# Waits between input loads, ten places apart, and a warm-up of many short matmuls in a long-convolution and MLP kernel

## The chip, the cores and the metric

The kernel runs on one core of one Trainium2 chip. The metric is the device time of one execution in microseconds, the median over several runs. A core has five instruction streams that run side by side and meet at semaphores: TensorE (PE; its weight loads are listed apart as PEld), VectorE (DVE), ScalarE (ACT), GpSimd (POOL) and SyncE (SP). SP computes nothing here; it issues DMA transfers, which 16 DMA engines carry out.

## What is computed

Two layers, each a gated long convolution (A) and an MLP (B), on a sequence of 2048 positions with 512 channels, in bf16:

```python
def _A_ref(q, k, v, shift_k, ssm_k, ssm_D):
    ...
    for t in range(ks):
        k_shift = k_shift + k_pad[:, t:t + S, :] * shift_k[:, ks - 1 - t][None, None, :]
    kv = k_shift * v
    ...
    y_f = kv_f * kf_f[None, :, :, :]
    ...
    y = y + kv * ssm_D[None, None, :]
    return q * y

def _B_ref(x, w1, b1, w2, b2):
    y = _layernorm(x, axis=-1)
    h = _gelu(jnp.einsum("bsd,df->bsf", y, w1) + b1)
    return jnp.einsum("bsf,fd->bsd", h, w2) + b2

x = A_q
x = x + _A_ref(_layernorm(x, axis=-1), A_k, A_v, A_shift_k, A_ssm_k, A_ssm_D)
x = x + _B_ref(_layernorm(x, axis=-1), B_w1, B_b1, B_w2, B_b2)
x = x + _A_ref(_layernorm(x, axis=-1), A_k, A_v, A_shift_k, A_ssm_k, A_ssm_D)
x = x + _B_ref(_layernorm(x, axis=-1), B_w1, B_b1, B_w2, B_b2)
```

`k_shift` is a causal filter of four taps along the sequence (ks = 4). `kv_f` and `kf_f` are Fourier transforms over a sequence padded to 4096, so y is the causal convolution of kv with ssm_k. It depends on k and v alone and is the same in both layers: the kernel computes it once.

## The kernel before

The program first makes a list of operations, each with an engine, a function that issues its instructions, and the operations that it depends on (`preds`, found from the memory that each reads and writes). `Prog.arrange` puts them in the order written out by hand in `ORDER`, engine by engine. `Prog.sync` turns dependences into semaphore waits, and leaves out those that an engine knows of already. `Prog.emit` issues everything: an instruction's waits come just before it on its engine, so a wait also holds back all that stands behind it in that engine's stream. A DMA that is waited for has a semaphore of its own.

The stages that the prediction speaks of, with their lines:

- **Loads.** ScalarE's queue issues four small ones (identity and first Fourier matrix, the taps, ssm_D). All others are on SP's queue: ssm_k in four pieces of 512 KB (L467), k in eight pieces of 256 KB (L482) and two small edge pieces (L474, L476), v in eight (L482), the second Fourier table in sixteen pieces of 256 KB (`tload`, L483), one small table (L490) and the row b2 (L703). `ORDER` puts these 40 first on SP, with no wait among them. Behind them stand sixteen copies from SBUF to SBUF (L577) that wait for the h2 stage, with b1 (L704) among them, and then the tables, q, W1 and W2 for the later stages, which overwrite memory that the first stages read. The last rows of W2 (L702) go to memory that nothing used before.
- **Warm-up** (L492 to L501, `warm`): GpSimd clears a 128x512 tile, and PE multiplies it by itself eight times, 512 columns each, into a PSUM tile that nobody reads. It is the first work on PE. The taps' matmuls (L511) and the transposes of ssm_k are made to follow it.
- **ht** (L522 to L534): PE transposes each quarter of ssm_k with 16 matmuls (L528), VectorE copies the result out of PSUM (`evac`, L453), and a small add on one row follows, on VectorE for two quarters and on GpSimd for two (L450).
- **h1, h2** (stage 1, L536; stage 2, L551): the transform of ssm_k, matmuls L545 and L558, evicted by ScalarE and VectorE.
- **fir** (L581 to L632): the filter of four taps. Channel groups 0 and 1 are done on PE: transposes of k (L589), then matmuls with diagonal matrices of the taps (L606), and a product with v on VectorE (L613). GpSimd makes the eight 128x128 diagonal matrices, one tap scaling each (L520), four for each group. In GpSimd's stream they stand behind the adds of the ht stage and two memsets (L489); their order is one of group 0, one of group 1, one of group 0, one of group 1, one of group 0, two of group 1, one of group 0. Group 1's matmuls come first on PE, so they need the first seven. Channel groups 2 and 3 are done on VectorE, as products and sums of two SBUF operands with 2048 columns (L450).
- **x1, x2, i1, i2**: the transform of kv (L545), the products with that of ssm_k (L651, matmuls of 64 columns; the products on VectorE), and the two inverse stages (L674, L731).
- **The layers** (L778 on): normalization on VectorE and GpSimd, the MLP on PE (L827, L860), GELU on ScalarE (L832), transposes by DMA (L807), stores.

PE's stream is fixed by `ORDER` too. Its beginning: warm-up, transposes of two quarters of ssm_k, tap rows, transposes of a third, h1 matmuls, transposes of the fourth, h1 with the transposes of k for group 1 and group 0 in between, the FIR matmuls of group 1, and then h2.

Of the kernel before, what the change touches and what calls it, by code (L numbers as in the profile page):

```python
# [12 lines left out]
PE, ACT, DVE, POOL, SP = "tensor", "scalar", "vector", "gpsimd", "sync"  # L13
# [25 lines left out]
class Prog:  # L39
# [157 lines left out]
    def arrange(self):  # L197

        self.order = {e: [] for e in (PE, ACT, DVE, POOL, SP)}
        last = [None] * 8  # L200
        second = set(self.SECOND)
        assert sorted(self.ORDER) == list(range(len(self.ops)))
        for at, i in enumerate(self.ORDER):
            o = self.ops[i]
            o.eng = o.engs[i in second]
            o.at, o.pos = at, len(self.order[o.eng])
            self.order[o.eng].append(o)
            tl = o.tile
            if tl is not None and tl.base is None:
                tl.base = self.BANKS[tl.i]  # L210
                for b in range(tl.base, tl.base + tl.nb):
                    if last[b] is not None:
                        for p in [p for p in last[b].ops if p.eng != PE] or last[b].ops[-1:]:
                            assert p.eng is not None
                            if p.i not in o.preds:
                                o.preds[p.i] = "psum"
                    last[b] = tl
            assert all(self.ops[p].eng is not None for p in o.preds)
# [149 lines left out]
def bass_interleave_layers__ssm_conv_h3__mixer_channel_mlp__prompt_kernel(  # L368
# [7 lines left out]
    def A(p0, n, off, *dims):  # L376
        return bass.AP(ar, p0 * AR + off, [[AR, n]] + [list(d) for d in dims])
# [7 lines left out]
    def Q(tile, p0, n, off, *dims):  # L385
        return bass.AP(ps, p0 * 4096 + tile.base * 512 + off, [[4096, n]] + [list(d) for d in dims])
# [65 lines left out]
    def evac(engs, dst, src, tile):  # L452
        f = {ACT: lambda e: e.activation(dst, src(), AF.Copy), DVE: lambda e: e.tensor_copy(dst, src())}  # L453
        return P.op(engs, f, writes=[dst], tile=tile)
# [14 lines left out]
    z = A(0, 1, R_K + c0, [512, 3], [1, WDV])  # L469
# [17 lines left out]
    for i in range(NPE):  # L487
        z = A(0, 128, R_KT[i], [130, 16], [1, 2])
# [3 lines left out]
    z = A(0, 128, R_W, [1, 512])  # L492
    P.op(POOL, lambda e, z=z: e.memset(z, 0.0), writes=[z])
    P.tag = "warm"
    tl = Tile(2)

    def f(e, tl=tl, z=z):
        for i in range(8):
            r = e.matmul(Q(tl, 0, 128, 0, [1, 512]), z[:, :128], z, start=True, stop=True)
        return r  # L500
    warm = P.op(PE, f, reads=[z], tile=tl)  # L501

    one = A(0, 1, R_ONE, [1, 128])
    P.op(POOL, lambda e: e.memset(one, 1.0), writes=[one])
    P.tag = "taps"
    tl = Tile(2)
    ins = [(i, A(0, 1, R_SR + 512 * c, [1, 512])) for i, c in enumerate(DV_CH)]

    def f(e, ins=ins, tl=tl):
        for i, m in ins:  # L510
            r = e.matmul(Q(tl, 0, 128, 512 * i, [1, 512]), one, m, start=True, stop=True)  # L511
        return r
    P.op(PE, f, reads=[one] + [m for _, m in ins], tile=tl).preds[warm.i] = "psum"
    for i in range(NDV):
        evac(ACT, A(0, 128, R_SJ + i * 512, [128, 4], [1, 128]), lambda tl=tl, i=i: Q(tl, 0, 128, 512 * i, [1, 4], [4, 128]), tl)
# [6 lines left out]
    for b in range(4):  # L522
        tl = Tile(2)
# [27 lines left out]
    def stage2(G, ks, n):  # L551

        tl = Tile(2)
        ins = [(i, A(0, 128, R_S2 + k * 128, [1, 128]), A(0, 128, G + k * n, [1, n])) for i, k in enumerate(ks)]

        def f(e):
            for i, w, m in ins:
                r = e.matmul(Q(tl, 0, 128, i * n, [1, n]), w, m, start=True, stop=True)  # L558
            return r
        P.op(PE, f, reads=[x for y in ins for x in y[1:]], tile=tl)  # L560
        return tl
# [5 lines left out]
    for k8 in range(16):  # L567
        tl = stage2(R_G, range(8 * k8, 8 * k8 + 8), 128)
# [203 lines left out]
    def ntmp():  # L772
        nn[0] += 1
        return R_N + (nn[0] % 8) * 512
# [3 lines left out]
    for L in range(2):  # L778
        s0 = 0
        for n in (BLOCKS0, BLOCKS1)[L]:  # L780
# [6 lines left out]
            for i, s in enumerate(sl):  # L787
                z = ntmp()
# [12 lines left out]
            for i, s in enumerate(sl):  # L801
                z = ntmp()
# [6 lines left out]
                tl = Tile(1)  # L809
# [9 lines left out]
            for fc in range(11):  # L819
                rows = 128 if fc < 10 else 96  # L820
                tl = Tile(1)
# [13 lines left out]
            for i, s in enumerate(sl):  # L835
                P.tag = "m2"
                tl = Tile(1)
# [63 lines left out]
```

## Time and profile before

| | |
|---|---|
| time of three runs | 242.47, 241.10, 241.46 us; median 241.46 |
| profiled execution, first to last instruction | 238.8 us |
| PE busy | 226.2 us (95%), 2312 matmuls, 2332 weight loads |
| DVE busy | 171.6 us (72%) |
| ACT busy | 138.3 us (58%) |
| POOL busy | 41.3 us (17%) |
| DMA | 27.40 MB, mean 115 GB/s; 241 to 383 GB/s over the first 30 us |
| instruction packets | 18 of 16 KB on one queue, 7 of 8 KB on another |

The profile is that of one execution on the chip. Its times count from the first instruction, and its span leaves out what lies before and behind the program; the median of the runs is 2.7 us longer. In its lists a row names the line of the kernel, the engine, the operation, what is written and read, and the shapes. Rows of a timeline merge instructions of one line that follow each other closely, with a count behind the x; idle time before a row stands in brackets with what ended it. The chain of waits is followed back from the last instruction: each piece is work, or a DMA, or "issue" where an engine waited for nothing that the profile shows. The ends of matmuls are modelled, so a PE that is busy 95% of the span isn't at its peak for all of it.

### The profile page before, as it was taken

How to read it: one execution, taken by the hardware profiler on the slowest of the kernel's cores; microseconds unless marked ns; L12 is line 12 of the kernel's file. 1: busy time of each engine (PE TensorE's matmuls, PEld its weight loads, DVE VectorE, ACT ScalarE, POOL GpSimd, SP SyncE). 2: the span in 40 equal slices, each digit the busy share in tenths (PEclk: the TensorE clock that was granted, in tenths of full speed). 3: DMA queues.
4: the chain of work that ended last, by engine and by line, in shares of the span. 5: the costliest groups of instructions: out<-in, count | busy, mean ns of one | idle time of the engine just before them, and what ended most of it. 6: DMA issues, size and time to landing. Idle time of an engine off the chain costs nothing.

```text
span 238.8 us, 5555 instructions
## 1 busy us (share of the span) xinstructions
PE 226.2 (95%) x2312; PEld 151.6 (63%) x2332; DVE 171.6 (72%) x359; ACT 138.3 (58%) x225; POOL 41.3 (17%) x77
## 2 busy tenths in 40 slices
PE   7987989886999999999999999999999999999995
PEld 3875778875899886766766667644444444444543
DVE  0979999999999999999887999693793312030035
ACT  2598799999999995642754444342782042454100
POOL 2179000000013444041230310400220200000000
PEclk9999999999999999999999999999999999999999
DMA  6999949999960003111122022240013021310024
GB/s 241 364 342 383 383 148 253 249 272 309 379 227 0 3 0 68 26 23 31 37 47 44 0 48 44 45 88 3 0 22 66 3 44 31 101 44 3 0 71 148
DMA packets 37035, 27.40 MB, mean 115 GB/s; under 512 B 19506, under 2 KB 29969, under 8 KB 37010
## 3 DMA queue, kind: packets, MB, share of 16 engines
q1 hardware_dynamic: 36446, 26.91, 37.8%
q8 instruction: 18, 0.29, 0.5%
q10 hardware_dynamic: 564, 0.14, 0.4%
q14 instruction: 7, 0.06, 0.1%
HBM read 16.82 MB, written 2.10 MB: 79 GB/s over the span
## 4 chain that ended last, share of the span: by engine, by line
PE 77%; ACT 9%; DMA 4%; DVE 4%; SPq 3%; issue 3%; ACTq 0%
PE ps L860 31%; PE ps L827 30%; ACT ar L453 9%; PE ps L674 5%; PE ps L731 3%; SPq L439 3%; PE ps L545 3%; DMA ar<-in_A_ssm_k_dram 2%; DVE ar L453 2%; DMA ar<-ar 2%; PE ps L528 1%; PE ps L606 1%; PE ps L849 1%; DVE sm L754 1%; PE ps L589 1%
## 5 line engine op out<-in xcount | busy, mean ns | idle before, releaser
L832 ACT ACTIVATE ar<-ps,sm 128x256 bf16<-128x256 f32 (+4 forms) x143 | 64.7, 525 | 72.5 <-PE ps L827 68.1
L827 PE MATMUL ps<-ar 128*128 128x256 bf16 (+4 forms) x568 | 84.2, 297 | 0.2
L860 PE MATMUL ps<-ar 128*128 128x512 bf16 (+1 forms) x329 | 79.0, 379 | 0.6
L453 ACT ACTIVATE ar<-ps 128x1024 bf16<-128x1024 f32 (+1 forms) x81 | 72.5, 1057 | 9.0 <-PE ps L511 4.5
L827 PEld LDWEIGHTS ps<-ar 128*128 128x128 bf16 (+1 forms) x572 | 52.9, 100 | 29.8 <-ACT ar L832 0.5
L450 DVE TENSOR_TENSOR ar<-ar 128x512 bf16<-128x512 bf16 (+3 forms) x106 | 63.6, 634 | 2.0 <-DMA ar<-in_A_k_dram 1.3
L860 PEld LDWEIGHTS ps<-ar 128*128 128x128 bf16 (+1 forms) x341 | 33.1, 98 | 34.3 <-ACT ar L832 0.3
L864 DVE TENSOR_TENSOR ar<-ar,ps 128x512 bf16<-128x512 bf16 x31 | 20.6, 680 | 47.3 <-PE ps L860 47.3
L754 DVE BATCH_NORM_STATS2 sm<-ar 128x6 f32<-128x512 bf16 (+1 forms) x68 | 42.8, 647 | 0.1
L768 DVE TENSOR_SCALAR ar<-ar,sm 128x512 bf16<-128x512 bf16 x64 | 25.0, 407 | 7.8 <-POOL sm L762 5.2
L760 POOL TENSOR_SCALAR sm<-sm 128x2 f32<-128x2 f32 (+2 forms) x26 | 6.0, 232 | 93.9 <-DVE sm L756 93.3
L762 POOL TENSOR_TENSOR sm<-sm 128x2 f32<-128x2 f32 (+2 forms) x26 | 21.6, 832 | 2.2
L545 PE MATMUL ps<-ar 128*64 128x128 bf16 x512 | 17.1, 221 | 1.4 <-issue 0.8
L545 PEld LDWEIGHTS ps<-ar 128*64 128x64 bf16 x512 | 14.9, 110 | 3.2 <-issue 1.0
L674 PE MATMUL ps<-ar 128*128 128x128 bf16 x256 | 15.0, 220 | 0.6 <-ACT ar L453 0.6
L674 PEld LDWEIGHTS ps<-ar 128*128 128x128 bf16 x256 | 14.7, 114 | 0.8 <-ACT ar L453 0.8
L453 DVE CAST ar<-ps 128x1024 bf16<-128x1024 f32 x11 | 13.0, 1212 | 0.3 <-PE ps L558 0.3
L651 PE MATMUL ps<-ar 128*128 128x64 bf16 x256 | 9.8, 194 | 3.2 <-ACT ar L453 2.7
L453 DVE COPY ar<-ps 128x2048 bf16<-128x2048 bf16 (+1 forms) x8 | 8.2, 1024 | 6.4 <-PE ps L528 6.3
L651 PEld LDWEIGHTS ps<-ar 128*128 128x128 bf16 x256 | 8.2, 98 | 4.7 <-ACT ar L453 3.9
L756 DVE BATCH_NORM_AGGREGATE sm<-sm 128x2 f32<-128x6 f32 (+1 forms) x64 | 9.9, 171 | 0.3
L558 PE MATMUL ps<-ar 128*128 128x128 bf16 x128 | 8.6, 220 | 0.8 <-ACT ar L453 0.8
(34 smaller groups left out, 78.1 us busy)
## 6 DMA issues: line engine op xcount, KB each, us to landing
ar<-tab_s SPq DMA_DIRECT2D x16, 256.0 KB, 9.6
ar<-ar SPq DMA_DIRECT2D x16, 256.0 KB, 4.2
ar<-in_A_ssm_k_dram SPq DMA_DIRECT2D x4, 512.0 KB, 5.3
ar<-in_A_k_dram SPq DMA_DIRECT2D x8, 256.0 KB, 7.6
ar<-in_A_v_dram SPq DMA_DIRECT2D x8, 256.0 KB, 9.6
ar<-in_A_q_dram SPq DMA_DIRECT2D x4, 512.0 KB, 7.9
out_dram<-ar SPq DMA_DIRECT2D x7, 256.0 KB, 2.1
ar<-in_B_w_dram SPq DMA_DIRECT2D x1, 1376.0 KB, 12.6
```

Source lines behind the costliest of these rows:

```text
L450: return P.op(eng, lambda e: e.tensor_tensor(o, a, b, op), reads=[a, b] + list(more), writes=[o])
L453: f = {ACT: lambda e: e.activation(dst, src(), AF.Copy), DVE: lambda e: e.tensor_copy(dst, src())}
L545: r = e.matmul(Q(tl, 64 * ri, 64, i * 128, [1, 128]), w, m, start=True, stop=True)
L651: r = e.matmul(Q(tl, 0, 128, i * pitch, [1, n]), w, m, start=True, stop=True)
L674: r = e.matmul(Q(tl, 0, 128, i * 128, [1, 128]), w, m, start=q == 0, stop=q == 1)
L754: P.op(DVE, lambda e, sj=sj, x=x: e.bn_stats(sj, x), reads=[x], writes=[sj])
L762: P.op(POOL, lambda e: e.tensor_tensor(r, v, hf, ALU.pow), reads=[v, hf], writes=[r])
L768: P.op(DVE, lambda e: e.tensor_scalar(o, x, m, r, ALU.subtract, ALU.mult), reads=[x, m, r], writes=[o])
L827: r = e.matmul(Q(tl, 0, rows, 0, [1, w]), a, m, start=dk == 0, stop=dk == 3)
L832: P.op(ACT, lambda e, dst=dst, tl=tl, rows=rows, bias=bias, w=w: e.activation(dst, Q(tl, 0, rows, 0, [1, w]), AF.Gelu_apprx_tanh, bias=bia ...
L860: r = e.matmul(Q(tl, 0, 128, 0, [1, 512]), ins[fc][0], ins[fc][1], start=fc == 0, stop=fc == 10)
L864: P.op(DVE, lambda e, x=x, tl=tl: e.tensor_tensor(x, x, Q(tl, 0, 128, 0, [1, 512]), ALU.add), reads=[x], writes=[x], tile=tl)
```

## The change

Two edits; the order of all operations stays.

```diff
@@ Prog.arrange
         second = set(self.SECOND)
         assert sorted(self.ORDER) == list(range(len(self.ops)))
+        early = [i for i in self.ORDER if self.ops[i].engs == (SP,) and self.ops[i].dma and not self.ops[i].preds]
+        for i, j in zip(early, early[10:]):
+            self.ops[j].preds[i] = "raw"
         for at, i in enumerate(self.ORDER):
@@ warm-up
     def f(e, tl=tl, z=z):
-        for i in range(8):
+        for i in range(6):
             r = e.matmul(Q(tl, 0, 128, 0, [1, 512]), z[:, :128], z, start=True, stop=True)
+        for i in range(60):
+            r = e.matmul(Q(tl, 0, 128, 0, [1, 64]), z[:, :128], z[:, :64], start=True, stop=True)
         return r
```

`early` is the list of DMAs on SP's queue that depend on nothing: the 40 loads at the head of the queue, then b1 (L704) and the last rows of W2 (L702), 42 in all. Each from the eleventh on now depends on the one ten places ahead, so that SP waits until that one has landed before it issues the next. The data, their order and their sizes are the same.

The warm-up keeps six of its eight matmuls of 512 columns and gets sixty of 64 columns, each with its own weight load of the same 128x128 zeros. PE's first operation thus issues 66 pairs of weight load and matmul instead of 8.

## The prediction

> **What bounds the kernel now.** I read the chain of waits first (start, length, what; one piece per row), because the change touches only the first 35 us and the chain says what those microseconds hang on.
>
> ```profile
> 1.18 4.84 DMA ar<-in_A_ssm_k_dram
> 6.03 0.05 issue
> 6.08 1.23 PE ps L528 x16
> ...
> 20.77 1.31 issue
> 22.08 1.01 PE ps L589 x15
> 23.09 0.05 issue
> 23.15 1.69 PE ps L606 x13
> 24.84 0.46 PE ps L558 x8
> 25.30 0.02 issue
> 25.32 10.20 ACT ar L453 x11
> ```
>
> The chain leaves the loads as early as 6.03 us and is compute afterwards: transposes (L528), first-layer matmuls, FIR matmuls (L606), ScalarE evictions. It has no load in it after the second ssm_k landing. So a slower load need not matter, and a later TensorE start can. Next the timeline of PE in the first microseconds (start, length, work).
>
> ```profile
> 1.56 3.33 PE L499 MATMUL ps<-ar 128*128 128x512 bf16 x8 [1.56 <-POOL ar L493]
> 4.78 2.52 PE L528 MATMUL ps<-ar 128*128 128x128 bf16 x32
> ```
>
> The eight zero matmuls end just as the first ssm_k load lands (4.73 us): the warm-up is hidden today with nothing to spare. Then the timelines of GpSimd and VectorE, which turn out to matter most.
>
> ```profile
> 13.86 2.70 POOL L520 TENSOR_SCALAR ar<-ar,sm 128x128 bf16<-128x128 bf16 x4
> ...
> 16.81 2.36 POOL L520 TENSOR_SCALAR ar<-ar,sm 128x128 bf16<-128x128 bf16 x1
> 19.26 0.60 POOL L520 TENSOR_SCALAR ar<-ar,sm 128x128 bf16<-128x128 bf16 x1
> 19.96 2.61 POOL L520 TENSOR_SCALAR ar<-ar,sm 128x128 bf16<-128x128 bf16 x1
> 22.67 1.22 POOL L520 TENSOR_SCALAR ar<-ar,sm 128x128 bf16<-128x128 bf16 x1
> ```
>
> ```profile
> 12.79 2.35 DVE L453 CAST ar<-ps 128x1024 bf16<-128x1024 f32 x2
> 16.42 2.36 DVE L450 TENSOR_TENSOR ar<-ar 128x2048 bf16<-128x2048 bf16 x2 [1.28 <-DMA ar<-in_A_k_dram]
> 18.70 1.22 DVE L453 COPY ar<-ps 128x2048 bf16<-128x2048 bf16 x1
> 19.83 3.58 DVE L450 TENSOR_TENSOR ar<-ar 128x2048 bf16<-128x2048 bf16 x3
> 23.34 1.21 DVE L453 COPY ar<-ps 128x2048 bf16<-128x2048 bf16 x1
> 24.87 1.23 DVE L613 TENSOR_TENSOR ar<-ps,ar 128x1024 bf16<-128x1024 f32 x1 [0.33 <-PE ps L606]
> ```
>
> A tap scaling (L520) takes 0.60 us while VectorE evicts PSUM, but 2.36 and 2.61 us when it is started during two-input SBUF products (L450): each time it ends about 0.45 us after two of these have passed (18.70 to 19.17, 22.10 to 22.57). Four scalings fit before VectorE's products begin at 16.42. The 16.42 is set by the 12th load, landing at 16.40. From there VectorE is busy to the end of the convolution:
>
> ```profile
> 16.40:26.00 9.60, 7.99 (x158) 6.76 (x153) 9.25 (x8) 7.02 (x8) 7.05 (x6) 1.00 1.05 380
> 26.00:40.00 14.00, 12.80 (x179) 10.36 (x179) 13.85 (x13) 14.00 (x16) 0.00 (x0) 1.00 0.81 240
> ```
>
> (Windows: length, then PE, PEld, DVE, ACT, POOL busy; clock, DMA share, GB/s.) Of 23.6 us VectorE is idle in 0.5, so what delays it there reaches the end.
>
> **The load waits.** They reorder nothing. On SP's queue the loads from the 11th on first wait for the landing of the load ten before. Landings lie 0.67 us apart (the table loads issued at 18.65 and 19.24 land at 28.13 and 28.80), which is 256 KB at the 380 GB/s of the windows: the DMA engines are full. The issue-to-landing time is 9.6 us (median of the table loads), so some 14 loads are in flight, and the wait cuts that to ten. The 11th and 12th loads are issued at 5.91 and 6.43, after the landings they now wait for (4.73, 6.03): no delay. The 13th moves from 6.91 to 7.37, later ones by 2 to 4.5 us, the 40th from 23.73 to about 27 (the 30th lands at 26.81). Queued behind them on SP are only further loads, then the copies of L577, which wait for ScalarE until 33.67: 6 us of cover. Does the queue run dry? Lower bound: the first load, alone, 512 KB, took 4.00 us from issue to landing, less than the 6.7 us that ten loads of 0.67 occupy: cost nothing. Upper bound: if a load kept needing 9.6 us, each would take 0.96 instead of 0.67, 28 loads 8.1 us, less the 1.75 us by which the tightest table load precedes its use (32.84 against 34.59): +6.4. I take **0**: the 9.6 is mostly queueing, which the window shortens, and the row without queueing is the 4.00. Two more waits (B_b1 at 34.45, W2's last rows at 50.27) are for loads landed by 28.13: 0. A gain is conceivable only through PE's instruction packets (below).
>
> **The warm-up.** Removed: two 512-column matmuls, 0.427 us each at their cold spacing. Added: 60 pairs of weight load and 64-column matmul. The nearest rows are the products of L651, the same form:
>
> ```profile
> 57.59 0.52 PEld L651 LDWEIGHTS ps<-ar 128*128 128x128 bf16 x16 [0.40 <-ACT ar L453]
> ```
>
> 16 loads of 98 ns in 0.52 us are 28 ns apart (matmul starts 29 ns) at full clock. Cold, by the 512-column rows (0.427 us, 0.83 ns a column), 64 columns are 53 ns. The record of the granted clock begins, at full rate, at 4.49 us. So: six matmuls from 1.56 end their issue at 4.09; 7 pairs at 53 ns to 4.49; 53 at 29 ns, 1.54 us; end 6.03, and the transposes start at about 6.05 instead of 4.78: **+1.27**. Bounds: all warm 60 x 0.029, end 5.83 (+1.05); all cold 60 x 0.053, end 7.29 (+2.5). I take +1.27, since the clock record lies inside the added run.
>
> [...]
>
> **Where that delay goes.** The chain behind the transposes is tight: VectorE's evictions (6.04, 7.34, 9.04), the next transposes (7.76, 10.39), the fourth eviction (11.65, 0.02 after its transposes). All move by 1.26. VectorE itself has cover: it idles 1.28 us before 16.42, so its products still start at 16.42 to 16.45. GpSimd has none: its queue has the small add after the fourth eviction (12.96), two memsets, then the eight scalings, all in order. Moved by 1.26, the scalings run thus: 15.12, 15.82 (ends 16.43), and the third asks at 16.52 where it was at 15.26, now after VectorE's products have begun.
> - 3rd: through two products, done 19.17 (as today's 5th).
> - 4th: 19.26 to 19.87, under the eviction of 18.70.
> - 5th: asked at about 20.1, through products, done 22.57 (as today's 7th).
> - 6th: asked 22.67, done 23.88 (as today's 8th).
> - 7th: 23.97 to 24.57, under the eviction of 23.34.
>
> The FIR matmuls of channel group 1 (L606, weight loads from 22.88) need the first seven scalings; today the seventh is done at 22.57. They would start at 24.62: 24.62 - 22.88 = **+1.74**, and end at 26.55 rather than 24.84. Behind them on PE stand the h2 matmuls (24.67), for which ScalarE waits; on VectorE, the product of 24.87. Both take the shift, about +1.7, and neither has slack: ScalarE's chain runs 10.2 us from 25.32. Copies, later loads and the MLP all hang on that work.
>
> **PE's instruction packets.** 58 more pairs are 116 more instructions. The page has 18 instruction packets of 16 KB for 4,644 PE records, 258 each, and PE stands 0.79 us at 14.81 and 1.31 us at 20.77 for nothing but "issue", about 256 instructions apart. I read these as waits for such packets. The boundaries move 116 instructions forward. Bounds: both gaps vanish, -2.1; one more like the larger, +1.3. I take **0**: even with the whole 1.27 added, the transposes before the FIR group end by 24.4 (23.09 now), ahead of the scaling at 24.57. Without that cover the change would read -2.1 to +1.3 plus the unabsorbed part of 1.27.
>
> **Sum.** 0 + 0 + 1.7: the profiled span goes from 238.8 to 240.5. The runs (median 241.46) hold 2.7 us around the span, so 241.46 + 1.7 = **243.2 us**.
>
> **Rivals.**
> - *The delay is absorbed* (the other side). [...] It decides below a shift of 0.46 (the fourth scaling, at 15.96, still ahead of 16.42) or with one-product waits. Against: both long rows passed two products. Chance 0.20. [...]
> - *Only one scaling is caught* (shift between 0.46 and 1.16): the seventh ends at 23.88, FIR starts at 23.93: +1.0, 242.5. Chance 0.08.
> - [...] Chance 0.12.
> - *The window drains the queue*: up to 247.9. Chance 0.05.
> - *Faster*: a shorter load queue lets PE's packets through and both gaps, 2.1 us, leave the chain: 239.4. Against: GpSimd gates the FIR. Chance 0.05.
>
> **Numbers.** The forecast has 0.50. About 0.5% (1.2 us) is what a measurement of this kernel tells from no change: faster means below 240.25, slower above 242.67. Slower: 0.50, 0.12, 0.05 and a little of the third case, 0.69; same: 0.26; faster 0.05. The range 241.2 to 244.6 takes in the absorbed case and the cold bound; the forecast's own is 242.6 to 243.8.
>
> **What would show it.** Right: transposes at 6.05; the third scaling long (2.4 to 2.7 us); FIR L606 starting near 24.6 behind GpSimd; VectorE idle about 2 us before L613; load landings within 0.2 us of today's. Wrong: landings more than 0.67 apart, pairs at 53 ns past 5 us, or FIR matmuls still at 22.9.

## The result, and the profile after

| | before | after |
|---|---|---|
| median of six runs each | 241.88 us (240.84 to 242.61) | 243.25 us (242.63 to 243.62) |
| ratio | | 1.0065, 95% interval 1.0036 to 1.0093 |
| profiled execution, first to last instruction | 238.8 us | 240.9 us |
| instruction packets on PE's queue | 18 | 19 |

The kernel became slower by 0.65%, 1.6 us of 241.88 (0.9 to 2.2 by the interval); the medians are 1.4 us apart. A ratio here is estimated from the single runs and is not the quotient of the two medians. The profiled execution after took 242.69 us by its own time, 1.8 us more than its span, and in every later run the time is 1.8 us above the span too.

The chain of waits after the change (start, length, what):

```profile
4.30 2.54 PE ps L504 x60
6.85 2.04 PE ps L533 x32
...
16.23 0.61 POOL ar L525
16.85 0.08 issue
16.93 2.54 POOL ar L525
19.55 0.61 POOL ar L525
...
20.41 2.46 POOL ar L525
22.87 0.08 issue
22.96 1.23 POOL ar L525
24.27 0.61 POOL ar L525
24.88 0.35 issue
25.23 1.69 PE ps L611 x13
26.92 0.46 PE ps L563 x8
27.40 10.20 ACT ar L456 x11
```

Lines have moved by three behind the load waits and by five behind the warm-up: L504 is the run of short matmuls, L533 the transposes, L525 the tap scalings, L611 the FIR matmuls, L456 ScalarE's evictions. Before, the chain from 20.77 to 23.15 was PE's own work behind an "issue" gap. Now it runs through seven scalings on GpSimd, two of them 2.5 us long. ScalarE's stretch of 10.20 us has the same length as before and starts 2.08 us later. The weight loads of the first FIR matmuls, before in the first row and after in the second:

```profile
22.88 1.73 PEld L606 LDWEIGHTS ps<-ar 128*128 128x128 bf16 x14
24.98 1.70 PEld L611 LDWEIGHTS ps<-ar 128*128 128x128 bf16 x14 [2.31 <-ACT ar L456]
```

They start 0.1 us after the seventh scaling is done (24.87). The bracket names ScalarE, but it is the scaling that ended just before.

The timeline of PE in the first microseconds:

```profile
1.56 2.74 PE L502 MATMUL ps<-ar 128*128 128x512 bf16 x6 [1.56 <-POOL ar L496]
4.10 2.75 PE L504 MATMUL ps<-ar 128*128 128x64 bf16 x60
6.68 2.21 PE L533 MATMUL ps<-ar 128*128 128x128 bf16 x32
```

The sixty pairs take from 4.10 to the first weight load of the transposes at 6.66, which is 1.88 us later than the 4.78 of before. The timeline of VectorE, where the new idle time shows in brackets:

```profile
16.73 2.35 DVE L453 TENSOR_TENSOR ar<-ar 128x2048 bf16<-128x2048 bf16 x2
18.99 1.21 DVE L456 COPY ar<-ps 128x2048 bf16<-128x2048 bf16 x1
20.13 3.58 DVE L453 TENSOR_TENSOR ar<-ar 128x2048 bf16<-128x2048 bf16 x3
23.63 1.21 DVE L456 COPY ar<-ps 128x2048 bf16<-128x2048 bf16 x1
26.95 1.23 DVE L618 TENSOR_TENSOR ar<-ps,ar 128x1024 bf16<-128x1024 f32 x1 [2.12 <-PE ps L611]
```

VectorE's products start 0.31 us later than before (16.73 against 16.42); its first FIR product, L618, starts 2.08 us later (26.95 against 24.87), after 2.12 us with nothing to do. The third scaling (16.93 above) was asked for just after the products began at 16.73, and came back two products later; the fifth (20.41) met the second group of products in the same way.

Two windows much like those of before (length, then busy PE, PEld, DVE, ACT, POOL; clock, DMA share, GB/s):

```profile
16.73:26.00 9.27, 6.08 (x139) 5.34 (x137) 8.11 (x8) 7.46 (x9) 8.21 (x8) 1.00 1.05 377
26.00:42.00 16.00, 14.79 (x206) 12.11 (x207) 14.99 (x13) 14.60 (x16) 0.00 (x0) 1.00 0.72 217
```

In the first window GpSimd is busy for 8.21 of 9.27 us, VectorE for 8.11 and PE for only 6.08; by the chain, GpSimd sets the pace here. The DMA engines are as full as before (share 1.05, 377 GB/s against 380). Matching the two traces operation by operation, PE's work is 2.1 us late at the FIR matmuls and 2.06 us late at the end of the program: the delay arises before 25 us and is carried unchanged through the rest.

### The profile page after: what moved, and what is told of

Read it like the earlier page. It is cut to its first block, busy times and chain, and to the rows that moved or that the text cites. A ratio compares the mean times of both kernels' runs of the same rounds, so it can differ in the third digit from the quotient of the medians.

```text
span 240.9 us, 5669 instructions
## 1 busy us (share of the span) xinstructions
PE 227.4 (94%) x2370; PEld 153.8 (64%) x2390; DVE 171.3 (71%) x359; ACT 138.2 (57%) x225; POOL 41.3 (17%) x77
## 4 chain that ended last, share of the span: by engine, by line
PE 77%; ACT 9%; POOL 4%; DVE 3%; SPq 2%; issue 2%; DMA 2%; ACTq 0%; POOLq 0%
PE ps L865 30%; PE ps L832 30%; ACT ar L456 9%; PE ps L679 5%; POOL ar L525 4%; PE ps L736 3%; SPq L442 2%; DMA ar<-ar 2%; PE ps L533 2%; PE ps L611 1%; PE ps L502 1%; PE ps L550 1%; PE ps L504 1%; DVE ar L456 1%; PE ps L854 1%
## 5 line engine op out<-in xcount | busy, mean ns | idle before, releaser
L456 ACT ACTIVATE ar<-ps 128x1024 bf16<-128x1024 f32 (+1 forms) x81 | 72.4, 1069 | 11.1 <-PE ps L516 6.1
L456 DVE COPY ar<-ps 128x2048 bf16<-128x2048 bf16 (+1 forms) x8 | 8.1, 1018 | 8.3 <-PE ps L533 8.3
L456 DVE CAST ar<-ps 128x1024 bf16<-128x1024 f32 x11 | 13.0, 1216 | 0.3 <-PE ps L563 0.3
```

## The experiments

The theory: the longer warm-up delays the transposes, that delays GpSimd's scalings into VectorE's products, and these delay the FIR matmuls; the load waits are neutral. Rivals: the load waits cost or gain something, the shifted instruction packets do, or the delay hurts through PE and not through GpSimd. Ratios are to the kernel before, run on the same chip at the same time.

**Each part alone.** The first kernel has the three lines of the load waits and the old warm-up.

```diff
+        early = [i for i in self.ORDER if self.ops[i].engs == (SP,) and ...]
+        for i, j in zip(early, early[10:]):
+            self.ops[j].preds[i] = "raw"
```

> Only the waits between the loads, with the old warm-up. Theory (the later start of PE pushes GpSimd's tap scalings under VectorE's two-input products; the load waits cost nothing): like the kernel before within 0.3%, the FIR matmuls L606 of group 1 start at 22.9 or somewhat earlier, the seventh scaling ends near 22.6, the loads land 0.67 us apart. Rival (the window drains the load queue, or moves the landings that VectorE waits for): about 0.6% slower, with landings wider apart than 0.67 us.

Measured: 241.82 us against 241.67, ratio 0.9989 (0.9956 to 1.0023). FIR started at 23.14, landings stayed 0.67 us apart. The weight loads around PE's gaps (idle time in brackets):

```profile
15.79 1.31 PEld L548 LDWEIGHTS ps<-ar 128*64 128x64 bf16 x45 [0.49 <-issue]
...
22.27 0.84 PEld L592 LDWEIGHTS ps<-ar 128*128 128x128 bf16 x15 [1.19 <-issue]
```

The load waits cost nothing that the time shows. The gaps for "issue", 0.95 and 1.44 us on the same engine before, became shorter, but only because PE came to them later: it went on 0.19 us later than before after both (15.79 and 22.27 against 15.60 and 22.08). The second kernel has the new warm-up alone.

```diff
-        for i in range(8):
+        for i in range(6):
             r = e.matmul(Q(tl, 0, 128, 0, [1, 512]), ...)
+        for i in range(60):
+            r = e.matmul(Q(tl, 0, 128, 0, [1, 64]), z[:, :128], z[:, :64], ...)
```

> Only the new warm-up, no waits between the loads. Theory: the whole loss, 0.6% (243.2 against 241.7), L606 of group 1 starts between 24.6 and 25.0, just after the seventh scaling. Rival (the load waits are the cause): within 0.2% of the kernel before.

Measured: 242.75 against 241.67, ratio 1.0021 (0.9991 to 1.0051). The ratio is short of the expected one and its interval takes in no change, so it is inconclusive. But nine of the 30 executions of before, and one of these 12, had a mean granted clock of 0.993 or less (on the clock, see the last section); the medians of the others are 241.56 and 242.75, 1.2 us apart. The trace is as expected: transposes at 6.48, the seventh scaling done at 24.45, FIR at 24.57.

```profile
24.57 1.70 PEld L608 LDWEIGHTS ps<-ar 128*128 128x128 bf16 x14 [1.51 <-issue]
```

**The delay without the instructions.** Fourteen matmuls of 512 columns in place of eight: twelve more instructions on PE, not 116, and about the same delay.

```diff
-        for i in range(8):
+        for i in range(14):
             r = e.matmul(Q(tl, 0, 128, 0, [1, 512]), ...)
```

> The kernel before with fourteen 512-column zero matmuls instead of eight, so that the transposes start between 6.0 and 6.8 as in the changed kernel, with 12 more instructions on PE instead of 116. Theory (the delay counts, not the number of instructions): 0.5 to 0.9% slower, L606 of group 1 near 24.6 to 25. Rival (the 116 instructions shift PE's instruction packets, and that is the loss): within 0.2% of the kernel before.

Measured: 243.7, ratio 1.0053 (1.0022 to 1.0084). Transposes at 6.53, the seventh scaling done at 25.20, FIR at 25.32.

```profile
25.32 1.70 PEld L606 LDWEIGHTS ps<-ar 128*128 128x128 bf16 x14 [0.60 <-issue]
```

So a delay of this size costs as much without the 116 instructions. This trace is not the changed kernel's in all: FIR is 0.34 us later than there, because a wait of PE for "issue" (1.15 us, before 17.34) held up VectorE's eviction at 20.01, and with it the second group of products; and the program ends 3.2 us later than before, with 0.8 us lost behind FIR.

**GpSimd alone.** The old warm-up and the old loads, and two more tap scalings ahead of the eight, into the zero tile of the warm-up, which nobody reads any more.

```diff
+    for _ in range(2):
+        d, t = A(0, 128, R_W, [1, 128]), M(0, 128, M_TAP, [1, 1])
+        P.op(POOL, lambda e, d=d, t=t: e.tensor_scalar(d, IDN, t, None, ALU.mult), ...)
```

> The kernel before, with two more tap scalings of 0.60 us, whose result nobody reads, in front of the eight on GpSimd; PE's warm-up and the loads are the old ones. Theory: GpSimd alone being 1.4 us later brings the loss: the third scaling is caught by VectorE's products, the seventh ends at 24 to 25, L606 of group 1 starts just after it, transposes still at 4.8: +1.3 to +2.2 us, ratio 1.005 to 1.009. Rival (PE's late start itself carries the delay): like the kernel before, ratio 0.998 to 1.002.

Measured: 244.8 against 241.9, ratio 1.009 (1.0051 to 1.0129). GpSimd's timeline, L872 being the two added scalings:

```profile
14.03 1.31 POOL L872 TENSOR_SCALAR ar<-ar,sm 128x128 bf16<-128x128 bf16 x2
15.44 4.37 POOL L520 TENSOR_SCALAR ar<-ar,sm 128x128 bf16<-128x128 bf16 x4
19.86 0.10 POOL L710 MEMSET sm<- 128x4 f32 x1
20.06 5.15 POOL L520 TENSOR_SCALAR ar<-ar,sm 128x128 bf16<-128x128 bf16 x4
```

and that of the weight loads:

```profile
22.09 0.84 PEld L589 LDWEIGHTS ps<-ar 128*128 128x128 bf16 x15 [1.53 <-issue]
...
24.63 1.70 PEld L606 LDWEIGHTS ps<-ar 128*128 128x128 bf16 x14 [1.69 <-issue]
```

PE's transposes of ssm_k started at 4.88 and its later transposes, L589, at 22.09, as before; still FIR started only at 24.63. The first four scalings took 4.37 us where they took 2.70, because the third ran from 16.84 to 19.11. The bracket puts the 1.69 us of idle time down to "issue", but the seventh scaling ended at 24.51: a wait for several semaphores is read from the end of the work it needs. So GpSimd alone brings a loss of this kind: 1.75 us at FIR and 2.06 at the end of the program. The size of the ratio is more than the delay: of the twelve executions seven had a mean granted clock of 0.993 or less, and the five others have a median of 242.79 (on the clock, see the last section).

**The cure.** If the order of the scalings is what carries the delay, the four that FIR group 1 needs can go first. Numbers in `ORDER` changed places:

```diff
-  91, 24, 56, 78, 85, 79, 86, 33, 59, 76, 89, 57, 87, ... 168, 60, 103, ... 182, 54, 169, 80, 61, 29, 183, 58, 199,
+  91, 24, 59, 78, 85, 79, 86, 33, 61, 76, 89, 60, 87, ... 168, 58, 103, ... 182, 56, 169, 80, 57, 29, 183, 54, 199,
```

With the whole change:

> The whole change, and in GpSimd's stream the four scalings of group 1 ahead of those of group 0; same instructions. Theory: the FIR of group 1 now needs the fourth scaling, which ends near 20.2, so it follows the transposes of group 0 directly, at 23 to 23.5; 1.2 to 1.9 us come back: 241.3 to 242.1. Rival (the delay of PE and ScalarE is passed on by themselves, whatever GpSimd does): 243.2, L606 still near 25.

Measured: 240.37 against 241.67, ratio 0.9916 (0.9882 to 0.995): faster than both kernels. The weight loads:

```profile
20.30 1.65 PEld L550 LDWEIGHTS ps<-ar 128*64 128x64 bf16 x57 [0.70 <-issue]
22.03 0.90 PEld L594 LDWEIGHTS ps<-ar 128*128 128x128 bf16 x16
22.89 1.73 PEld L611 LDWEIGHTS ps<-ar 128*128 128x128 bf16 x14
```

FIR follows the transposes without a gap, at 22.89 instead of 24.98, although this execution's first transposes began even later than in the changed kernel (7.21). The third scaling is again caught (17.47 to 20.00); the fourth, the last that FIR needs, is done at 20.69. The 2.09 us by which FIR starts earlier answers most of the 2.9 us between the medians of the two kernels (243.25 and 240.37, which were not measured side by side).

With the kernel before:

> The kernel before, with only the new order of the tap scalings (group 1's four first). Theory: before the change the scalings end just ahead of the FIR's other inputs (22.57 against 22.9), so the order is worth at most 0.3 us here: ratio 0.997 to 1.001. Rival (the order alone explains the 0.8% by which the whole change with the new order beats the kernel before): ratio near 0.992, L606 of group 1 starting before 22.5.

Measured: 241.22 against 241.9, ratio 0.9973 (0.9949 to 0.9998). FIR is at 23.02, no earlier than before (22.88), so the 0.3% was not won there; against the 22 executions of before with a mean granted clock of 0.999 or 1 (median 241.43) it is 0.2 us. The rest of the gain needs the change as well. With the new warm-up and the new order, without the load waits:

> The new warm-up and the new order of the scalings, without the load waits. Theory (the load waits cost and bring nothing): the same as the whole change with the new order, 240.0 to 240.8, ratio 0.990 to 0.995. Rival (the load waits bring part of that, by letting PE's instruction packets through): near 241.5, with a longer idle time of PE between 18 and 23 us.

Measured: 241.52, ratio 0.998 (0.9955 to 1.0004).

```profile
21.45 1.65 PEld L547 LDWEIGHTS ps<-ar 128*64 128x64 bf16 x57 [1.75 <-issue]
23.18 0.90 PEld L591 LDWEIGHTS ps<-ar 128*128 128x128 bf16 x16
24.04 1.73 PEld L608 LDWEIGHTS ps<-ar 128*128 128x128 bf16 x14
```

The same 57 weight loads, with 1.75 us of "issue" ahead of them and not 0.70. PE's second instruction packet started on its DMA engine at 18.89 here, at 17.74 with the load waits. FIR is 1.15 us later than with the load waits, and the medians differ by 1.15 us (241.52 and 240.37, from two chips). The expectation that the load waits bring nothing fell; its rival held: once the scalings were out of the way, the packet started 1.15 us sooner with the shorter load queue. The size rests on one profile of each. With the old order of the scalings the same comparison gives less: the packet started at 17.51 with the load waits and at 17.80 without, and PE went on at 20.04 and at 20.42.

With the load waits and the new order, but the old warm-up:

> The load waits and the new order of the scalings with the old warm-up. What is asked: which of the three parts a kernel that beats both needs. If VectorE's start (12th load near 16.5) and PE's instruction packets decide once GpSimd is out of the way: L606 of group 1 at 22.5 to 23.2, 240.2 to 241.3, ratio 0.992 to 0.998. If the new warm-up itself is needed (its 116 instructions put the packet boundaries in a better place): 241.2 to 241.8, no better than the order alone (0.9973), with PE idle for 'issue' twice between 14 and 23 us.

Measured: 241.77 against 241.67, ratio 0.9987 (0.9956 to 1.0018). FIR at 22.79, with PE's weight loads idle for "issue" for 0.83 us near 15.2 and 0.68 near 21.3. The new warm-up is needed too, though by FIR's start alone this kernel is no worse than the best; it lost about 1 us near 129 us, where PE waits 0.73 us for an addition on VectorE; why is not explained. The same with waits seven places apart:

> As the one before, with waits for the load seven places ahead instead of ten. If a shorter load queue lets PE's instruction packets through (the idle times of PE for 'issue' near 14.5 and 21 us shrink from 0.6 and 1.3 to below 0.5 together) and seven loads still fill the DMA engines (landings 0.67 us apart): 0.2 to 0.6% faster than with ten. If seven are too few: landings 0.7 us or more apart, the last near 35 to 36 instead of 34, the time up to 0.5% longer than with ten.

Measured: 241.98, ratio 1.0016 (0.9987 to 1.0046). The DMA issues between 14 and 28 us (KB each, median us from issue to landing), first with ten places,

```profile
ar<-tab_s SPq DMA_DIRECT2D x13, 256.0 KB, 6.1
```

then with seven:

```profile
ar<-tab_s SPq DMA_DIRECT2D x12, 256.0 KB, 4.7
```

Each load lands sooner, but the last one at 36.28 and not 34.11: with seven loads in flight the DMA engines were idle now and then (295 GB/s in this stretch against 359). PE's second wait for "issue" was gone, as hoped, and FIR began earliest of all here, at 21.90; it brought nothing.

**The place of the packets.** Sixty short matmuls alone, no long ones: 104 more instructions than before, about the same end of the warm-up, no load waits.

```diff
-        for i in range(8):
-            r = e.matmul(Q(tl, 0, 128, 0, [1, 512]), ...)
+        for i in range(60):
+            r = e.matmul(Q(tl, 0, 128, 0, [1, 64]), z[:, :128], z[:, :64], ...)
```

> The warm-up as sixty 64-column matmuls alone, none of 512 columns, no load waits: 104 more instructions on PE, but they end near 4.6 to 4.8 us (53 ns apart until the clock is released, 29 after), so that the transposes start with the landing of the first load as before. Theory (delay counts, not instructions): GpSimd's scalings as before, L606 of group 1 at 22.5 to 23.1, ratio 0.996 to 1.002. Rival (the shifted instruction packets cost time): ratio 1.004 or more. If the shifted packets save time later on, below 0.996.

Measured: 243.37 against 241.9, ratio 1.0053 (1.0026 to 1.0079). This is a miss: no loss was expected.

```profile
21.21 1.48 PEld L545 LDWEIGHTS ps<-ar 128*64 128x64 bf16 x51 [2.64 <-issue]
22.78 0.89 PEld L589 LDWEIGHTS ps<-ar 128*128 128x128 bf16 x16
23.63 1.73 PEld L606 LDWEIGHTS ps<-ar 128*128 128x128 bf16 x14
```

The transposes (4.87) and the seventh scaling (22.75) are as before. PE waited 2.64 us in one gap, its packet having started only at 18.66, and FIR moved by 0.75 us, from 22.88 to 23.63. Here nothing covers the wait, and it shows. Eight of the twelve executions also had a lower granted clock, so the kernel was profiled once more:

> The sixty 64-column matmuls alone once more, for a profile of an execution whose mean granted clock is 0.993, as in 8 of 12 runs of it. If the missing 0.7% is the clock falling to half for one stretch of 3.4 us while PE waits near 18 to 25 us: the clock's row shows it there, matmuls after it 107 ns apart instead of 56, and about 2 us more than the 240.4 of the first profile. If the clock is merely released later at the start: it shows before 10 us.

The windows of this second profile (columns as above, the clock third from the end):

```profile
17.77:21.18 3.41, 1.28 (x27) 1.01 (x24) 3.41 (x4) 2.30 (x3) 3.07 (x5) 1.00 1.05 384
21.18:24.59 3.41, 3.34 (x56) 3.17 (x57) 2.66 (x3) 2.20 (x3) 3.04 (x2) 0.50 1.06 383
24.59:28.00 3.41, 3.41 (x46) 2.87 (x45) 2.03 (x2) 2.04 (x3) 0.00 (x0) 1.00 1.05 381
```

After a stretch in which PE was busy for 1.28 of 3.41 us, its clock was halved for 3.41 us. PE worked through 56 matmuls in that stretch where the first profile has 75, FIR started at 25.20, and the time was 243.75 against 242.31 in the first profile. So the miss has two parts: the wait for the packet, and a slow stretch of the clock after it, seen in this profile and likely in the eight executions with a lower clock. That the wait brings the slow stretch is not shown (last section).

Last, the best kernel with thirty short matmuls for sixty:

> The whole change with the new order of the scalings, but thirty 64-column matmuls instead of sixty. The transposes should start at 5.0 to 5.7 instead of 7.2. If VectorE's later start (17.26 there) is what holds that version now: VectorE's products start at 16.4 to 16.9, L613 at 24.7 to 25.1 instead of 25.29, 239.9 to 240.4, ratio 0.988 to 0.992. If the place of PE's packet boundaries matters more, and 60 fewer instructions move one into a worse place: L606 at 23.3 or later behind a wait for issue of over 1.3 us, ratio 0.995 or more.

Measured: 241.25 against 241.55, ratio 0.9975 (0.9944 to 1.0006). The transposes began at 5.31, 1.9 us earlier than with sixty, yet FIR started 0.8 us later:

```profile
21.92 0.81 PEld L550 LDWEIGHTS ps<-ar 128*64 128x64 bf16 x27 [0.90 <-issue]
22.82 0.90 PEld L594 LDWEIGHTS ps<-ar 128*128 128x128 bf16 x16
23.68 1.73 PEld L611 LDWEIGHTS ps<-ar 128*128 128x128 bf16 x14
```

PE's weight loads waited 1.67 us for "issue" near 13.9 and 0.90 near 21.0. Neither the earlier start nor the 60 instructions fewer helped. The rival holds, by which the sixty matmuls serve the best kernel through the place of the packet boundaries; they can do so because the scalings no longer gate FIR there.

## Why the prediction was right, and where its sizes were off

- **The load waits, 0.** Right for the change as it stands: alone they measured 0.9989, landings stay 0.67 us apart, and a table load takes 6.3 us from issue to landing where it took 9.6. So at least 3.3 of the 9.6 us were queueing, which the prediction read as most of it. Its sign "within 0.2 us of today's" was too narrow: the last load lands at 33.94 against 33.49, though the chain of waits has no load there. Its last load issue, 27.25, is the "about 27" of the prediction.
- **The warm-up, +1.27: mis-sized, +1.88.** The prices of a pair were right: the trace has about 34 pairs 53 ns apart and about 25 of 29 ns. What failed is the sentence that the clock record, at 4.49, "lies inside the added run" and so fixes how many pairs are slow. The full clock came at 5.93 in this execution, after 34 pairs and not 7: 4.10 + 34 x 0.053 + 25 x 0.029 = 6.63. That moment differed among kernels with the same warm-up (last section). Later than predicted, but short of the cold bound (end at 7.29, +2.5). The chance of 0.12 was for pairs that stay slow to the end; the slow pairs measured are 53 ns apart, as in that bound. In the two profiles with the same warm-up and the new order the pairs were slow to the end, or nearly: with the load waits about 58 of the sixty, without them all, and the transposes began at 7.21 and 7.26. So this term had a spread of 0.8 us over four profiles with the same warm-up (6.48, 6.66, 7.21 and 7.26).
- **Two scalings are caught.** Right in the place and the mechanism: the third and the fifth are long (2.54 and 2.46 us; 2.65 and about 2.5 by the forecast), the sixth takes 1.23, and the fourth and the seventh, under the evictions, take 0.61 us. The start of FIR was forecast at 24.62 and measured 24.98: VectorE's fourth eviction came 1.67 us late (13.32 against 11.65), more than the 1.28 us of idle time that was to cover it, so the products began at 16.73, right behind the evictions and not with the 12th load (16.49). So **+1.74 was mis-sized too, +2.1**, as a consequence of the later start.
- **The absorbed case**, in which a scaling comes back after one product and not two, fell: both long scalings passed two products. The sixth, asked for during the last product of its group (22.96), came back when that one was over (24.17). In one other profile, the second of the sixty short matmuls alone, a scaling asked for 0.03 us ahead of the products came back after one (16.73 to 18.37), so two is not a fixed number. Why a scaling started among the products takes 2.54 and 2.46 us and not 0.61, and comes back mostly after two of them, no run shows.
- **The packets, 0.** Right: the added scaling wait covers them, as the kernels with the new warm-up alone and with fourteen long matmuls show by the seventh scaling standing right before FIR (24.45 and 24.57, 25.20 and 25.32). The price without that cover was given as -2.1 to +1.3 and the rest; the sixty short matmuls alone measured +0.75 in the trace.
- **No slack behind FIR.** Right: 2.1 us late at FIR, 2.06 at the end.
- **The sum.** 1.7 us was forecast; the two traces differ by 2.06 us, the medians by 1.4. Those differ because "the 2.7 us around the span" was two things: 1.8 us that lie around the span in every run, and 0.9 us by which the profiled execution of before (238.8 + 1.8 = 240.6) was quicker than its median. That 243.2 hits 243.25 so closely is luck. Its base, the median of three runs, lies 0.4 us below that of six (241.46 against 241.88), and its step lies 0.3 us above that of the medians (1.7 against 1.4): the errors had opposite signs.

What stays open: the best kernel's profiled span is the same 238.8 as that of before, whose profile is one of its quickest executions. The 0.8% is a result of the times, and part of it is the clock (last section); the runs show what the order does for the changed kernel (2.09 us at FIR) and what the load waits add (1.15 us in one pair of profiles), but no profile of a typical execution of before shows where its last microsecond goes.

## What to carry to other kernels

Follow a delay into every engine's own queue, not only down the one that it starts on: 1.9 us on TensorE was made up by TensorE itself (the transposes ahead of FIR end at 22.7, at 22.9 before), and cost 2.1 us because small GpSimd operations slid behind long two-operand SBUF products on VectorE (2.54 and 2.46 us each instead of 0.61). Put the small operations that the next stage needs first, so that being caught costs nothing; that made the same change worth -0.8% (-0.5% against the executions of before at full clock) instead of +0.65%. An edit that brought nothing alone (the load waits, 0.9989) came with a gain of 1.15 us once the bound had moved (241.52 and 240.37, from two chips), so try it again after the bound is removed.

## What the runs showed of the hardware

- **The moment of the full clock varies.** With PE working from 1.56 us on in every kernel, the record of the full clock began at 4.34, 4.49, 4.89, 4.90, 5.53, 5.65, 5.93, 6.54, 7.14 and 7.53 us in different profiles: a spread of 3.2 us. What sets the moment is not shown. The half-clock stretch above (clock 0.50 from 21.18 to 24.59) came after 3.41 us with PE 38% busy. But in the first profile of the same kernel PE was busy for only 0.96 of the same 3.41 us (17.77 to 21.18), and in the changed kernel for 1.17 of the 3.41 us from 22.99 on, and in both the clock stayed full. So what decides the fall is not shown either.
- **A lower mean clock goes with a longer time.** One such stretch makes a mean granted clock of 0.993 (half of 3.41 in 241.9 us). Executions with a mean of 0.986 to 0.996 are longer by about 1.6 to 2 us: of the kernel before 9 of 30, 13 of 35, 8 of 23 and 6 of 17 executions, with medians 242.9 to 243.6 against 241.2 to 241.6 for the others. Of the best kernel it was none in 7, of the kernel before with the new order of scalings none in 12. It is not the order alone: with the old order it was none in 12 for the fourteen long matmuls and one in 12 each for the load waits alone and the new warm-up alone. What keeps the clock up was not tried. Against the other executions of before alone (241.56), the best kernel is 1.2 us faster, so the gain is not only this.
- **Instruction packets came later with more loads in flight.** A packet of 16 KB for PE takes about 0.9 to 1.4 us, and seems to hold up one DMA engine: in the kernel before a packet ran from 13.01 to 14.11; 15 of the 16 parts of the 11th load had landed by 13.93, the last at 15.23, and the last part stays behind in the loads that follow. So the 12th load, on which VectorE's products waited before, was there but for one part at 14.70, and landed at 16.40; the next load of 256 KB, there but for one part at 15.88, landed at 17.20. PE stands for "issue" ahead of about the 449th of its records in eight of the 14 traces, and ahead of the 705th, 256 further on, in 13, whatever instruction is there; each time it goes on 2.4 to 2.6 us after the packet started. In four pairs of kernels that differ in the load waits alone, the next packet started 3.6 to 4.9 us after PE came to the 705th record with the waits, 5.4 to 6.0 us without. With nine to fifteen loads in flight the runs show waits of 0.5 to 2.64 us there.
- Some profiles lose 0.3 to 1.0 us late: near 95 us, where PE waits for a DMA inside SBUF (1.0 us with waits seven places apart, 0.34 with fourteen long matmuls), or near 130 us, where it waits for an addition on VectorE (0.82 and, with ten places and the old warm-up, 0.73). It was not tried, and is open.
